# A linear-attention and soft-MoE kernel: combinations four row groups at a time, other PSUM banks in the tail, one DRAM row for k, q, v, and another order

## The chip, the cores and the metric

The kernel runs on one core of a Trainium2 chip. The core has TensorE (PE in the profile, with PEld for its weight loads), VectorE (DVE), ScalarE (ACT), GpSimd (POOL) and SyncE (SP), which here issues every DMA. The metric is the device time of one execution in microseconds (us); lower is better.

## The reference

Two computations follow each other. The first is a gated linear attention over 4 batches, 8 heads, 768 steps and 48 channels; the second is a soft mixture of 8 experts with 4 slots each, over the 3072 rows of 384 channels that the first gives.

```python
B, H, S, D = q.shape                       # 4, 8, 768, 48
f = 1.0 / (1.0 + np.exp(-f_logit))
for t in range(S):
    state = f[:, :, t, :, None] * state + np.einsum('bhd,bhe->bhde', k[:, :, t], v[:, :, t])
    y[:, :, t] = np.einsum('bhd,bhde->bhe', q[:, :, t], state)
x = y.transpose(0, 2, 1, 3).reshape(B * S, H * D)        # 3072 x 384
...
logits = x @ phi                                          # 3072 x 32
d = softmax over rows (columns of slots normalised);  slot_input = d.T @ x
for e in range(E):
    h = np.maximum(slot_input[e] @ w1[e], 0.0)            # 4 x 384 @ 384 x 1024
    slot_out[e] = h @ w2[e]                               # 4 x 1024 @ 1024 x 384
c = softmax of logits over the 32 slots
return c @ slot_out                                       # 3072 x 384
```

Everything is in 32-bit floats.

## The kernel before

**The loop.** The sequence is cut into 24 blocks, `n`, of 128 steps of one batch (6 time blocks times 4 batches, the four batches next to each other). All 8 heads of a block go through together. For each pair of blocks the gates are made: ScalarE exponentiates and takes a logarithm (`exp`, `ln`), VectorE sums logarithms by a scan (`scan`, lines 478 and 479), and ScalarE exponentiates the sum twice (`g` at line 492, `p` at 493). Each block multiplies keys by `g` (`mk`, line 515) and queries by `p` (`mq`, 518). On PE follow: four transposes of the keys (`tk`, 523) with a copy (`pk`, 526), keys by values (`kv`, 544) from which VectorE makes the next state (`sa` 548, `sm` 553), queries by state (`ie`, 563), scores (`sc`, 532), a triangular mask on VectorE (`mask`, 535), masked scores by values (`ia`, 572), a copy of the result (`py`, 575), four transposes (`tx`, 603) and another copy (`px`, 606). After every four blocks a "unit" gathers the logits of 512 rows (line 621), updates a running maximum and the slot sums (lines 625 to 656; the transposes at 642 and their copies at 646 among them).

**After the loop.** The last maxima of four partition groups are joined (724 to 758), the slot inputs are formed (743), and the expert part begins: 12 `up` products of 4 column groups (779), a ReLU (785, 787), 4 groups of four transposes (`tn`, 794) with a copy that masks (800), 12 `down` products in three parts `p` of 128 output channels (`dn`, 813), for each part a scaling (`po`, 821), a sum over head groups (`so`, 825) and a copy (`ps`, 829). Then come the combinations `cb`: for each part, slot outputs by the row softmax for the 3072 rows. A combination of before, `cb{p}{x}`, makes two products, each on 32 rows of the array: partition groups 0 and 32 for even `x`, 64 and 96 for odd `x`. Each result (128 x 768 floats) is copied out (`pf`, 842) and stored (`st`, 845). There are 4 per part, 12 in all. PE also gets idle-time products: `warm` ahead of the loop (417) and `fill` near the end (731).

**Memory.** PSUM is eight banks: three pairs (`pr0` for scores, `pr1` and `pr2` for block results) and two singles (`sg0`, `sg1`) that serve everything of kind "one", the up, turn and down results among it; combinations use the pairs. In SBUF, k, q and v have four buffers each, logits' sums `f` three and decays `c` two groups of two blocks, masked scores two. `w1` is loaded in 12 pieces of 1 MB into `homes` during the loop, paced by the blocks. `w2` has 12 pieces too: three go to homes, seven to the loop's buffers when these come free (`ARENA`), two to homes that the up products have read.

**What sets the order.** A planner (`Plan`, lines 131 to 275) is run while the program is built. Each operation has an estimated time, a priority and, where the table `ENGINE` (line 124) says so, a fixed engine; `LATER` (81) adds to its priority. The planner repeatedly takes the operation that can start first; starts within `WINDOW` of each other count as equal and the priority decides. The program is then written out in that order, and each engine works its list in order. SP too works its DMA list in order: one that waits holds all behind it. Operations with two SBUF operands on VectorE and all on GpSimd are kept from running side by side by explicit waits (lines 937 to 943).

A last operation reads a flag and would run a general, slow path (`general`) if gates were extreme; with these inputs it doesn't run.

Of the kernel before, what the change touches and what calls it, by code (L numbers as in the profile page):

```python
# [16 lines left out]
BT = 128  # L17
# [17 lines left out]
NHOME = 15  # L35
# [37 lines left out]
def t_scan(n):  # L73
# [6 lines left out]
WINDOW = 0.21  # L80
LATER = {
# [5 lines left out]
    "fill": (12.5, 2.9, 4, 21.4, 18.1, 18.3, 19, 14.9), "flag": (0, -14.4, 0.6, -14.5, -18.7, -18.7, -18.7, -18.7),  # L87
# [20 lines left out]
    "scan": (16.7, 12.4, 11.5, 22.8, 22.8, 19.2, 25, 22.8), "sex": (23.7, -22.8, 15.1, 0, 7.3, 7.3, 7.3, 7.3),  # L108
    "si": (-10.5, 0, 0, 0, -23.4, -23.4, -23.4, -23.4), "siv": (13.2, -3.3, 1, 0, -2.2, -2.2, -2.2, -2.2),
    "sm": (-6.5, 16.2, -22.7, 20.8, -10.1, -15.1, 6.1, 2.3), "sml": (-13, 23.5, 8.2, 0, 16.8, 16.8, 16.8, 16.8),  # L110
    "smx": (10, -11.1, -15.3, 0, -10.3, -10.3, -10.3, -10.3),
# [6 lines left out]
    "twb": (-21, 0, 0, 0, -24.1, -24.1, -24.1, -24.1), "twd": (-20.2, 0, 0, 0, -23, -23, -23, -23),  # L118
# [4 lines left out]
}  # L123
# [7 lines left out]
class Plan:  # L131
# [7 lines left out]
    LAT, PE_LAT, SWITCH, DMA_LAT, RATE, DEPTH = 0.13, 0.17, 0.19, 2.0, 375e3, 8  # L139

    INS, PAGE, FETCH = 4, 256, 5.8
# [7 lines left out]
    def add(self, name, eng, fn, r=(), w=(), psum=None, kind=None, prio=0.0, bytes=0, after=(), two=False, form=None, products=0):  # L149

        op = dict(name=name, eng=eng, fn=fn, psum=psum, kind=kind, prio=prio, bytes=bytes, n=len(self.ops), two=two, form=form, products=products)
# [23 lines left out]
    def schedule(self):  # L175
# [24 lines left out]
        while ready:  # L200
            best = None
            for n in ready:
# [8 lines left out]
                for e, us in sorted(op["eng"].items()):  # L211
# [4 lines left out]
                    if e == "SP":  # L216
                        t = max(t, landed[-self.DEPTH])
                    elif e == "POOL" or (op["two"] and e == "DVE"):
                        t = max(t, port if holder == e else port + self.LAT)
                    elif e == "PE" and op["form"] != form:  # L220
                        t = max(t, free.get(e, 0.0) + self.SWITCH)
                    if own is None or t + us < own[1]:
                        own = (t, t + us, op["prio"], n, e)
                if best is None or self.better(own, best):
# [3 lines left out]
            op = ops[n]  # L228
            if e == "PE":
# [10 lines left out]
            if e == "SP":  # L240
                pipe = max(pipe, t + self.DMA_LAT) + op["bytes"] / self.RATE
                end = pipe
                landed.append(end)
# [826 lines left out]
```

## Time and profile before

| | us |
|---|---|
| median of 3 runs | 170.55 |
| lowest and highest run | 169.25 and 171.65 |
| the profiled execution | 169.53 |
| span of its profile | 167.8 |

The profile is of one execution. Its span goes from the first to the last instruction, 1.7 us less than the time of that execution. "Busy" is the time in which an engine had an instruction under way. Matmuls are pipelined, so the mean length of one is longer than the distance to the next; a float product is two passes, and an entry "x4" of PE in the chain counts instructions of that kind. The granted clock is TensorE's, 1.00 for full speed; over this execution it was 0.994 on the mean.

### The profile page before, as it was taken

Reading aid. Unit: us, or ns where it says so; the run is one execution under the profiler, and the core shown is the slowest. Engines: PE = TensorE matmul, PEld = TensorE weight load, DVE = VectorE, ACT = ScalarE, POOL = GpSimd, SP = SyncE. Lnnn points to the kernel's source line nnn. Section 1 sums busy time; section 2 is a strip of 40 time slices with the busy share of each in tenths; the row PEclk is TensorE's granted clock in tenths of the full one; section 3 lists DMA queues with packets and bytes.
Section 4 is the critical chain, followed back from the end, with each engine's and each line's share of the span. In section 5 each row is a group of like instructions: output and inputs, shape, how many; then the busy total and the mean of one; then the engine's idle time right before and its main releaser. Section 6 shows DMA issues by size and latency. Waiting matters only on the chain.

```text
span 167.8 us, 5887 instructions
## 1 busy us (share of the span) xinstructions
PE 153.7 (92%) x2477; PEld 116.3 (69%) x2477; DVE 123.6 (74%) x239; ACT 97.5 (58%) x182; POOL 25.1 (15%) x41
## 2 busy tenths in 40 slices
PE   2998999999999999999999999999989998999940
PEld 2987777688787887788777887787532276857530
DVE  6889979899999999999999999994660162233420
ACT  4998976878689797937985786543302100131300
POOL 3002020230306030321128131500000000000000
PEclk9999999999999999999999999999999999999997
DMA  5999999999999999999999968179999990536680
GB/s 164 349 406 384 407 429 388 355 327 398 395 377 352 355 341 379 364 378 400 401 381 293 357 231 274 68 256 424 422 424 424 410 383 27 191 144 262 241 294 23
DMA packets 17604, 54.02 MB, mean 322 GB/s; under 512 B 1952, under 2 KB 5152, under 8 KB 14496
## 3 DMA queue, kind: packets, MB, share of 16 engines
q1 hardware_dynamic: 17568, 53.55, 84.2%
q8 instruction: 21, 0.34, 0.9%
q14 instruction: 15, 0.12, 0.2%
HBM read 48.82 MB, written 4.72 MB: 319 GB/s over the span
## 4 chain that ended last, share of the span: by engine, by line
PE 63%; DVE 13%; ACT 7%; DMA 7%; issue 3%; SPq 1%; POOL 1%; DVEq 0%; POOLq 0%; ACTq 0%
PE pr L532 11%; PE sg L813 7%; PE sg L779 6%; PE pr L572 6%; PE pr L563 6%; PE sg L603 5%; PE pr L836 5%; DMA ak<-in_k_dram 4%; DVE as L535 4%; PE sg L621 3%; PE sg L523 3%; DMA aq<-in_q_dram 3%; PE sg L650 2%; PE sg L544 2%; ACT ac L493 2%
## 5 line engine op out<-in xcount | busy, mean ns | idle before, releaser
L535 DVE TENSOR_TENSOR as<-pr,tri 128x1024 f32<-128x1024 f32 x24 | 29.2, 1215 | 2.1 <-PE pr L532 1.4
L532 PE MATMUL pr<-aq,ak 48*128 48x128 f32 x384 | 27.9, 285 | 0.4 <-DVE as L535 0.2
L532 PEld LDWEIGHTS pr<-aq,ak 48*128 48x128 f32 x384 | 23.3, 187 | 5.0 <-issue 2.6
L572 PE MATMUL pr<-as,av 128*48 128x128 f32 x384 | 24.1, 274 | 1.1 <-DVE as L535 1.0
L572 PEld LDWEIGHTS pr<-as,av 128*48 128x48 f32 x384 | 20.2, 123 | 2.8 <-DVE as L535 2.0
L603 PE MATMUL sg<-ident,xT 128*128 128x128 f32 x96 | 15.2, 283 | 0.4 <-ACT ag L526 0.2
L518 POOL TENSOR_TENSOR aq<-aq,ac 128x512 f32<-128x512 f32 x9 | 11.4, 1281 | 25.0 <-DMA aq<-in_q_dram 8.7
L575 ACT COPY xT<-pr 128x512 f32<-128x512 f32 x20 | 11.6, 581 | 5.6 <-PE pr L572 5.4
L563 PE MATMUL pr<-aq,st 48*48 48x128 f32 x320 | 13.5, 279 | 0.2 <-DVE aq L518 0.2
L493 ACT ACTIVATE ac<-ac 128x1024 f32<-128x1024 f32 (+1 forms) x13 | 12.9, 993 | 0.5
L515 POOL TENSOR_TENSOR ak<-ak,af 128x512 f32<-128x512 f32 x6 | 7.7, 1281 | 35.4 <-ACT af L492 35.3
L603 PEld LDWEIGHTS sg<-ident,xT 128*128 128x128 f32 x96 | 10.4, 141 | 3.6 <-issue 1.5
L523 PE MATMUL sg<-ident,ak 128*128 128x128 f32 x80 | 11.9, 282 | 0.0
L478 DVE TENSOR_TENSOR_SCAN ac<-chain,af 128x256 f32<-128x256 f32 x16 | 10.9, 682 | 1.0 <-issue 1.0
L526 ACT COPY ag<-sg 128x512 f32<-128x512 f32 x17 | 9.4, 585 | 3.2 <-PE sg L523 3.2
L606 ACT COPY xr<-sg 128x384 f32<-128x384 f32 x17 | 8.1, 480 | 5.3 <-PE sg L603 5.2
L842 DVE COPY hm<-pr 128x768 f32<-128x768 f32 x6 | 5.7, 958 | 7.0 <-PE pr L836 7.0
L563 PEld LDWEIGHTS pr<-aq,st 48*48 48x48 f32 x320 | 8.3, 119 | 3.5 <-issue 2.0
L479 DVE TENSOR_TENSOR_SCAN ac<-chain,af 128x256 f32<-128x256 f32 x16 | 10.7, 667 | 0.0
L779 PE MATMUL sg<-hm,si 128*32 128x512 f32 x96 | 10.5, 593 | 0.1
L544 PEld LDWEIGHTS sg<-av,ag 128*48 128x48 f32 x320 | 8.6, 124 | 2.7 <-issue 1.2
L842 ACT COPY hm<-pr 128x768 f32<-128x768 f32 x6 | 4.8, 799 | 9.8 <-PE pr L836 9.8
(129 smaller groups left out, 254.2 us busy)
## 6 DMA issues: line engine op xcount, KB each, us to landing
hm<-in_w_dram SPq DMA_DIRECT2D x17, 1024.0 KB, 8.1
ak<-in_k_dram SPq DMA_DIRECT2D x24, 256.0 KB, 6.5
aq<-in_q_dram SPq DMA_DIRECT2D x24, 256.0 KB, 6.1
av<-in_v_dram SPq DMA_DIRECT2D x24, 192.0 KB, 5.8
out_dram<-hm SPq DMA_DIRECT2D x12, 384.0 KB, 2.6
af<-in_f_dram SPq DMA_DIRECT2D x7, 512.0 KB, 6.0
ag<-in_f_dram SPq DMA_DIRECT2D x4, 512.0 KB, 6.1
af<-in_w_dram SPq DMA_DIRECT2D x1, 1024.0 KB, 7.0
```

The costliest lines, as they stand in the source:

```text
L493: add(f"p{n}", {"ACT": t_act(w)}, lambda e: nc.scalar.activation(flat(c_), flat(c_), AF.Exp, scale=-1.0), w=cs, prio=T(n, 1.2))
L518: tt(e)(flat(q_), flat(q_), flat(c_), op=ALU.mult)
L523: nc.tensor.transpose(pk[:, a], k_[:, a], ident)
L532: nc.tensor.matmul(ps[:, r, a], k_[rows[r], col(a)], queries(r, a), start=True, stop=True)
L535: tt(e)(sc_.rearrange("p r (m x) t -> p (r m) (x t)", x=2), bank(("sc", n)).rearrange("p r (m t) -> p (r m) t", m=2), tri.rearrange("p x t ...
L544: nc.tensor.matmul(pk[rows[r], col(a)], kp_[:, col(a), rows[r]], v_[:, 2 * a + r], start=True, stop=True)
L563: nc.tensor.matmul(py[at : at + D, r, a // 2], s0[rows[r], col(a)], queries(r, a), start=a < 2, stop=False, skip_group_check=True)
L572: nc.tensor.matmul(py[at : at + D, r, a // 2], v_[:, 2 * a + r], sc_[:, r, a], start=first and a < 2, stop=a >= 2, skip_group_check=True)
L575: copy(e)(xT[:, n % NXT].rearrange("p (r m) t -> p r (m t)", r=2), bank(("y", n))[:, :, : 2 * BT])
L603: nc.tensor.transpose(px[:, i], xT[:, n % NXT, i], ident)
L779: nc.tensor.matmul(ph[32 * qq : 32 * qq + 32], si[:, c], t[:, qq], start=c == 0, stop=c == 2, skip_group_check=True)
L813: nc.tensor.matmul(po[32 * qq : 32 * qq + 32, :w], hT[:, j, 4 * kh + kk, 32 * qq : 32 * qq + 32], t[:, qq, kk], start=(j, kh, kk) == (0, 0 ...
```

## The change

The diff does six things.

1. **Combinations.** A combination now makes four products on all four row groups into one tile of four banks (`halves_`), two of them per part. It has two copies and two stores, as many stores in all as before. All but the last combination use the tile `halves_[1]`; the last uses `halves_[0]`.
2. **Banks in the tail.** PSUM is now two tiles of four banks. The names `pairs` and `ones_` are views of them, in the same sizes as before. The planner gets further pools over the same memory: "late" (the four banks of the second tile) and "spare" (two of the first). Up and turn results may be in "one", "late" or "spare", down results and head sums in "one" or "spare". `fill` is done 4 times in place of 12, from `ident`.
3. **k, q, v.** Host code puts them side by side into one DRAM row of 1408 floats per partition. From block 4 on one DMA loads all three; for blocks 0 to 3 k and q come together and v by itself. There are five buffers for them, four groups of `f`, three of `c` and three of masked scores.
4. **Memory for that.** Two homes fewer (13): one piece of `w2` goes to a home ahead and nine to the loop's buffers. `phi` is loaded over `ones`, once warm-up and `tri` have read it; `wd` and `si` lie over `tri`. The pieces of `w1` and of that first `w2` are loaded in halves, paced over all blocks.
5. **The planner's costs.** Form changes of PE have a price for each form, DMAs a price by row length, some products another length, instruction pages two prices; sums and combinations may be taken 0.3 ahead.
6. **The order.** `WINDOW` is 0, and `LATER` and `ENGINE` are new tables. By `ENGINE` the keys' product `mk` is on GpSimd for all blocks from 4 on (an "A" that an operation can't use leaves the choice to the planner).

```diff
-NHOME = 15
+ROW = 2 * PR * BT + DM
+NHOME = 13
...
-WINDOW = 0.21
+WINDOW = 0
 LATER = {
...
 ENGINE = {
-    "ends": "AA--DDDD", "mk": "--DP-PDA", "mq": "AA--D---", "pc": "PD-PDA--", "pe": "-PA-----", "pf": "AA-AD-P-",
-    "pk": "-AA--P--", "plt": "--D-PPPP", "ps": "D---PPPP", "px": "D-APA-PP", "py": "A-APPPA-", "relu": "AD--PPPP",
-    "sml": "A-------", "ssb": "DPD-DDDD",
+    "ends": "-A--DAAA", "mk": "APADPPPP", "mq": "-PA-PAAP", "pc": "PAPP----", "pe": "ADPPPPPP", "pf": "-P-DAAAP",
+    "pk": "A--AA-AA", "pl": "DP-PDPDD", "plt": "A-AAPAAA", "ps": "AAP-AAAA", "px": "--AP-PDA", "py": "-AP-----",
+    "relu": "-P--AAAA", "sml": "PPP-AAAA", "ssb": "DPP-PPPP",
...
-    LAT, PE_LAT, SWITCH, DMA_LAT, RATE, DEPTH = 0.13, 0.17, 0.19, 2.0, 375e3, 8
+    LAT, PE_LAT, DMA_LAT, DEPTH = 0.13, 0.17, 2.0, 8
+    SWITCH = {"turn": 0.07, "col": 0.1, "row": 0.2, "half": 0.22, "slot": 0.16, "comb": 0.1, "sum": 0.1, None: 0.1}
...
-    pairs = [pp.tile([128, 2, 512], F32, tag=f"pr{i}", name=f"pr{i}") for i in range(3)]
-    ones_ = [pp.tile([128, 512], F32, tag=f"sg{i}", name=f"sg{i}") for i in range(2)]
-    plan = Plan({"sc": [0], "pair": [1, 2], "one": [0, 1]})
+    halves_ = [pp.tile([128, 4, 512], F32, tag=f"pq{i}", name=f"pq{i}") for i in range(2)]
+    pairs = [halves_[0][:, :2], halves_[1][:, :2], halves_[1][:, 2:]]
+    ones_ = [halves_[0][:, 2], halves_[0][:, 3]]
+    plan = Plan({"sc": [0], "pair": [1, 2], "one": [0, 1], "late": [0, 1, 2, 3], "spare": [0, 1], "quad": [1], "last": [0]})
...
-    NF, NK, NQ, NV, NSS, NXT = 3, 4, 4, 4, 5, 6
+    NF, NC, NB_, NSC, NSS, NXT = 4, 3, 5, 3, 5, 6
...
-    phs = part(AV, 1920, 128, a=PR)
+    phs = ones.rearrange("p (a s) -> p a s", a=PR)
...
-        load(kb[n % NK], k[n], f"k{n}", [("k", n % NK)], T(n, -9), 262144)
-        load(qb[n % NQ], q[n], f"q{n}", [("q", n % NQ)], T(n, -8.5), 262144)
-        load(vb[n % NV], v[n], f"v{n}", [("v", n % NV)], T(n, -7), 196608)
+        for name, x in (("kq", slice(0, 1024)), ("v", slice(1024, ROW))) if n < 4 else (("kqv", slice(0, ROW)),):
+            load(bb[n % NB_][:, x], kqv[n, :, x], f"{name}{n}", [("b", n % NB_, c) for c in name], T(n, -7 if name == "v" else -8.5))
...
-        def combine(p, x):
+        def combine(p, h):
             def fn(e):
-                for y in range(2):
-                    gs = slice(64 * (x % 2) + 32 * y, 64 * (x % 2) + 32 * y + 32)
+                for y in range(4):
+                    gs = slice(32 * y, 32 * y + 32)
                     nc.tensor.matmul(
-                        bank(("cb", p, x))[:, y, :384], s4[gs, CUT[p] : CUT[p + 1]], cts[gs, 3 * (x // 2) : 3 * (x // 2) + 3], start=True, stop=True,
+                        bank(("cb", p, h))[:, y, :384], s4[gs, CUT[p] : CUT[p + 1]], cts[gs, 3 * h : 3 * h + 3], start=True, stop=True,
                     )
...
-    add("phs", {"SP": 0.42}, lambda e: nc.sync.dma_start(phs, phi), w=["phs"], prio=T(0, 1), bytes=65536)
+    add("phs", {"SP": 0.42}, lambda e: nc.sync.dma_start(phs, phi), w=["phs", "ones", "warm"], prio=T(0, 1), dma=0.3)
...
-        for x in range(4):
-            h = x // 2
-            add(f"cb{p}{x}", {"PE": 0.4}, combine(p, x), r=[("s4", p), *[("cts", 3 * h + y) for y in range(3)]], psum=("cb", p, x), kind=("pair", "sc"), prio=tp + 2 + 0.1 * x, form="comb", products=2)
...
+        for h in range(2):
+            last = (p, h) == (NPART - 1, 1)
+            add(f"cb{p}{h}", {"PE": 0.65}, combine(p, h), r=[("s4", p), *[("cts", 3 * h + y) for y in range(3)]], psum=("cb", p, h), kind=("last",) if last else ("quad",), prio=tp + 2 + 0.1 * h, form="comb", products=4, ahead=0.3, after=[*ps, *others] if last else ())
+            for x in (2 * h, 2 * h + 1):
+                add(f"pf{p}{x}", {"ACT": t_act(768), "DVE": t_dve(768, True)}, put_f(p, x), psum=("cb", p, h), w=[("st", p, x)], prio=tp + 2.5 + 0.1 * x, after=sdeps[p][x])
```

More of the change, by code (lines that the diff above doesn't have):

```diff
@@ L228, in schedule @@
             op = ops[n]
+            t += op["ahead"]
             if e == "PE":
@@ L278, in gla_soft_moe_kernel @@
 @with_exitstack
-def gla_soft_moe_kernel(ctx: ExitStack, tc: tile.TileContext, q, k, f, v, fd, qd, kd, vd, phi, w1, w2, out):
+def gla_soft_moe_kernel(ctx: ExitStack, tc: tile.TileContext, f, kqv, fd, qd, kd, vd, phi, w1, w2, out):
     nc = tc.nc
@@ L581, in block @@
         if not final:
-            add(f"tk{n}", {"PE": 0.4}, turn_k, r=[K, "ident"], psum=("kt", n), kind=("one",), prio=T(n, 3), form="turn", products=4)
+            add(f"tk{n}", {"PE": 0.48}, turn_k, r=[K, "ident"], psum=("kt", n), kind=("one",), prio=T(n, 3), form="turn", products=2)
             add(f"pk{n}", {"ACT": t_act(512), "DVE": t_dve(512, True)}, put_k, psum=("kt", n), w=[KP], prio=T(n, 3.5))
@@ L672, in unit @@
         for w_ in (1, 0):
-            add(f"te{u}", {"PE": 0.11}, tr(w_), r=[("et", "lt")[w_], "ident"], psum=("el", u, w_), kind=("one",), prio=t0 + 0.6 - 0.1 * w_, form="turn", products=1)
-            add(f"pe{u}", {"ACT": 0.28, "DVE": 0.25}, put_e(w_), psum=("el", u, w_), w=[(("el",), ("ltok", u))[w_]], prio=t0 + 0.8)
-        add(f"pi{u}", {"PE": 0.42}, pins, r=[("el",), *[("x", (n0 + g) % NX) for g in range(UB)]], psum=("pi", u), kind=("one",), prio=t0 + 1, form="slot", products=4)
+            kind = ("e", "l")[w_]
+            add(f"t{kind}{u}", {"PE": 0.2}, tr(w_), r=[("et", "lt")[w_], "ident"], psum=("el", u, w_), kind=("one",), prio=t0 + 0.6 - 0.1 * w_, form="turn", products=0.5)
+            add(f"p{kind}{u}", {"ACT": 0.28, "DVE": 0.25}, put_e(w_), psum=("el", u, w_), w=[(("el",), ("ltok", u))[w_]], prio=t0 + 0.8)
+        add(f"pi{u}", {"PE": 0.62}, pins, r=[("el",), *[("x", (n0 + g) % NX) for g in range(UB)]], psum=("pi", u), kind=("one",), prio=t0 + 1, form="slot", products=4)
         add(f"pp{u}", {"DVE": t_dve(384, True)}, put_p, r=[AL] if u else [], psum=("pi", u), w=["pin"], prio=t0 + 1.2)
@@ L706, in slots @@
         for u in (2 * th, 2 * th + 1):
-            add(f"ct{u}", {"PE": 0.11}, turn(u), r=[L, "ident"], psum=("ct", u), kind=("one",), prio=sp + 0.5, form="turn", products=1)
+            add(f"ct{u}", {"PE": 0.2}, turn(u), r=[L, "ident"], psum=("ct", u), kind=("one",), prio=sp + 0.5, form="turn", products=0.5)
             add(f"pc{u}", {"ACT": 0.28, "DVE": 0.25}, put(u), psum=("ct", u), w=[("cts", u)], prio=sp + 0.6)
@@ L730, in fill @@
         def fill(e):
-            nc.tensor.matmul(bank("fill")[:, 0, :128], ones, ones, start=True, stop=True)
+            nc.tensor.matmul(bank("fill")[:, :128], ident, ident, start=True, stop=True)
         def t_wb(e):
@@ L763, in tail @@
         last = plan.w[("bank", ("lg", L))]
-        for x in range(12):
-            add(f"fill{x}", {"PE": 0.2}, fill, r=["ones"], w=[("bank", "fill")] if x else [], psum="fill", kind=None if x else ("sc",), prio=t0 + 50, form="sum", products=1, after=[last])
+        for x in range(4):
+            add(f"fill{x}", {"PE": 0.2}, fill, r=["ident"], w=[("bank", "fill")] if x else [], psum="fill", kind=None if x else ("spare",), prio=t0 + 50, form="sum", products=1, after=[last])
         add("twb", {"ACT": 0.2}, t_wb, r=["zr1", ("nm", L)], w=["wb"], prio=t0)
-        add("twd", {"DVE": 0.15}, t_wd, r=["wb", "same"], w=["wd"], prio=t0)
+        add("twd", {"DVE": 0.15}, t_wd, r=["wb", "same"], w=["wd", "tri"], prio=t0)
         add("psi", {"PE": 0.21}, psi, r=["wd", "pin"], psum="psi", kind=("one",), prio=t0, form="slot", products=12)
@@ L850, in tail @@
                     x = W1.index((j, hf, c))
-                    add(f"up{j}{hf}{c}", {"PE": 0.86}, up(j, hf, c), r=["si", ("home", x)], w=[("bank", ("up", j, hf))] if c else [], psum=("up", j, hf), kind=None if c else ("one",), prio=t0 + 1 + 0.1 * x, form="slot", products=4)
+                    add(f"up{j}{hf}{c}", {"PE": 0.86}, up(j, hf, c), r=["si", ("home", x)], w=[("bank", ("up", j, hf))] if c else [], psum=("up", j, hf), kind=None if c else ("one", "late", "spare"), prio=t0 + 1 + 0.1 * x, form="slot", products=4)
                 H_ = ("hs", 2 * j + hf)
@@ L917, in gla_soft_moe_kernel @@
         sdeps[p] = [home_deps(x) for x, o in at]
+    ps, others = [], [plan.w["flag"], plan.w["bank", "fill"], *[plan.w["cts", u] for u in range(NU)]]
     for p in range(NPART):
```

138 lines of the change are left out of this document (75 added, 63 removed), and 71 rows, old and new, of the table LATER.

## The prediction

> **What bounds the kernel now.** I read the page first, then the windows by stage, then the chain of waits in order of time, and last the timeline where the chain changes engine.
>
> ```profile
> span 167.8 us, 5887 instructions
> ...
> PE 153.7 (92%) x2477; PEld 116.3 (69%) x2477; DVE 123.6 (74%) x239; ACT 97.5 (58%) x182; POOL 25.1 (15%) x41
> ```
>
> The page says that TensorE (PE) is busy for 92% of the span. That is a mean over unlike stages, so I cut the span where the work changes: until the first scores, until a full flow, the loop, the joint to the expert part, the up products, the turns, the down products, the end, the run-out. Columns: length, then busy us of PE, weight loads, VectorE (DVE), ScalarE (ACT), GpSimd (POOL), then granted clock, DMA share, GB/s.
>
> ```profile
> 0.00:9.60 9.60, 6.50 (x33) 6.38 (x33) 7.03 (x18) 6.90 (x14) 1.67 (x13) 1.00 0.80 279
> 9.60:18.88 9.28, 7.99 (x118) 6.56 (x117) 8.42 (x14) 8.63 (x15) 1.28 (x1) 1.00 1.06 398
> 18.88:112.46 93.58, 92.31 (x1624) 74.17 (x1624) 88.97 (x162) 71.36 (x134) 22.11 (x27) 1.00 0.93 341
> 112.46:123.08 10.62, 9.74 (x139) 6.98 (x135) 6.93 (x25) 3.27 (x10) 0.00 (x0) 1.00 1.01 424
> 123.08:133.51 10.43, 10.43 (x96) 3.01 (x96) 1.98 (x6) 1.40 (x3) 0.00 (x0) 1.00 1.01 420
> 133.51:136.47 2.96, 2.51 (x21) 1.68 (x17) 1.98 (x3) 0.60 (x1) 0.00 (x0) 1.00 1.01 421
> 136.47:154.19 17.72, 17.23 (x420) 13.18 (x419) 5.05 (x9) 3.46 (x5) 0.00 (x0) 1.00 0.45 177
> 154.19:161.15 6.96, 6.96 (x46) 4.33 (x42) 3.22 (x4) 1.86 (x3) 0.00 (x0) 1.00 0.66 254
> 161.15:167.80 6.65, 0.00 (x1) 0.00 (x0) 0.00 (x0) 0.00 (x0) 0.00 (x0) 0.85 0.30 105
> ```
>
> In the loop (93.58 us) PE lacks work for only 93.58 - 92.31 = 1.27 us; DVE is close behind with 88.97. An order can win there only by making the PE work itself shorter, or by 1.27. In the up stage PE is never idle. The rest has slack of another kind: chains of small steps, and combinations.
>
> The chain of waits for the back (start, length, engine and line; L794 turns, L813 down products, L825 head sums, L821 and L829 their copies, L836 combinations; pieces between are left out):
>
> ```profile
> 134.36 0.67 PE sg L794 x4
> 135.87 0.66 PE sg L794 x4
> 136.53 3.69 PE sg L813 x128
> 140.24 0.36 DVE xT L821
> 140.64 0.50 PE sg L825 x2
> 141.17 0.30 DVE xT L829
> 141.51 1.56 PE pr L836 x8
> ...
> 146.70 0.84 PE pr L836 x4
> ...
> 147.97 1.49 PE pr L836 x8
> ...
> 150.47 1.03 PE pr L836 x8
> ...
> 154.26 0.84 PE pr L836 x4
> ...
> 155.97 1.52 PE pr L836 x8
> ```
>
> One old combination is x4 (two products of two passes, two row groups). Its price differs: 0.84 alone, 1.49 to 1.56 for most pairs, but 1.03 for the pair at 150.47.
>
> **Part 1, the combinations, before the last down product.** The old code gives combination x rows 0-63 or 64-127 by x's parity, so a neighbouring pair can occupy all four row groups, which is what one new combination does by design. The pair at 150.47 is therefore the nearest row for it: 1.03. A lower end is 0.84, what two groups cost, if the other two run wholly beside them; an upper end is 1.52, if nothing overlaps. Between 136.47 and 154.19 stand seven old combinations: 1.56 + 0.84 + 1.49 + 1.03 = 4.92 us. There will be four new ones (two each of parts 0 and 1, the seven and the one that now comes at 154.26): at the middle of 0.84 and 1.03, 4 x 0.94 = 3.8. Saved 1.1, between 4.92 - 4 x 0.84 = 1.6 and 4.92 - 4 x 1.52 = -1.2.
>
> The Trainium skill ("TensorE: Matmul & The Clock Gate", Part 3) gives two figures: a span of one matmul plus 4 ns for each further tile, and a measured 3.07 times for four row tiles. By the first a new combination would cost 0.84 and part 1 save 1.6; by the second four products take 1.3 times one (0.65 by 1.49 - 0.84, so 0.85, and the same 0.2 of switching ahead: 1.04) and it saves 0.8. The pair at 150.47 speaks for the second.
>
> From 140.24 to 141.51 lie 0.36 + 0.30 us of DVE copies and about 0.1 at each handover, with only two small transposes of PE work beside them. With down products of part 1 there instead (their weights: part 3 below), about 0.8 is hidden; one or two more returns to the down form cost 0.2. Term A: 1.1 + 0.8 - 0.2 = 1.7; bounds -1.2 and 2.4.
>
> **Part 2, after the last down product.** Here the stores answer, not the combinations.
>
> ```profile
> out_dram<-hm SPq DMA_DIRECT2D x12, 384.0 KB, 2.6
> 159.00:160.00 1.00, 1.00 (x8) 0.46 (x6) 0.33 (x1) 0.80 (x1) 0.00 (x0) 1.00 1.01 396
> 159.67 0.96 DVE L842 COPY hm<-pr 128x768 f32<-128x768 f32 x1 [1.18 <-PE pr L836]
> L842 ACT COPY hm<-pr 128x768 f32<-128x768 f32 x6 | 4.8, 799 | 9.8 <-PE pr L836 9.8
> ```
>
> Before: last down product ends at 154.26, last copy at 159.67 + 0.96 = 160.63, its store lands 2.6 later, at 163.2, or 9.0 after the down product. The remaining 4.6 us to 167.80 hold no engine work and stay. After: copy 0.36, sum 0.50, copy 0.30, handovers 0.3: the first new combination starts 1.5 later and ends at 2.4, ScalarE copies 0.8, to 3.3. From then four stores of 393 KB follow each other, at the 396 GB/s that a full DMA second shows 0.99 us each: 3.3 + 2.6 + 3 x 0.99 = 8.9. By the engines alone it would be 2.4 + 0.94 + 0.96 + 2.6 = 6.9. Term: 0.1, bounds -0.5 and 2.1.
>
> **Part 3, from the up products to the down products.** The up products end at 133.5, the down products start at 136.47. Of the 2.96 us between, four groups of turns take 2.51 busy; they run there because the up results held the two single banks. With six more banks for up and turn results, three groups of turns can go between up products and three of part 0's four down products before the last turn. The turns remain PE work, now with a form change more each way. I take 0.7 saved; bounds 0 and 1.6 (0.45 idle, and the 1.1 that overlapping turns with each other showed as 0.67 each).
>
> The weights of the down products must keep up:
>
> ```profile
> 100.72 0.33 SPq L440 DMA_DIRECT2D af<-in_w_dram  x1
> ...
> 125.92 2.04 SPq L440 DMA_DIRECT2D hm<-in_w_dram  x2
> ```
>
> Two homes less means one piece of w2 loaded early instead of three, but before, too, the first piece of w2 went out at 100.72 and the last two at 125.92, and the DMA ran at 420 GB/s to 136.47. The same 12 MB follow the loop, spots in the same number; the last two are used near 151. Cost 0; should they come 10 us later, the PE would wait for what exceeds 15.
>
> **Part 4, the joint (10.62 us, PE idle 0.88).** One wait there is the order's:
>
> ```profile
> 119.95 0.14 PEld L642 LDWEIGHTS sg<-ident,av 128*128 128x128 f32 x1 [0.26 <-DVE zr L727]
> ```
>
> The transpose that feeds the slot sums waits for the bank of another small product, though its exponentials are done. A new order may shed that: 0.4, bounds -0.5 and 0.9. Twelve filling products become four; they fill waits, cost 0, and if their cover goes, each costs under 0.2.
>
> **Part 5, the loop.** Arithmetic, shapes and counts are unchanged. What an order changes are PE's form changes:
>
> ```profile
> 48.75 0.59 PE sg L523 x4
> 49.33 0.44 PE sg L603 x4
> ```
>
> Four transposes take 0.59 behind another form and 0.44 behind transposes: 0.15 a merge. There are 44 such groups (20 of keys, 24 of outputs), so 22 merges, some of them there already, are at most 3.3 us; the score and state products can hardly pair up, with one bank pair for scores. Adding the 1.27 idle, the upper bound is 4.5; the lower is -1.5, an order that merges less. A third copy of scores and of decays and a fifth of k, q, v give freedom, as does DVE, which sheds work:
>
> ```profile
> L515 POOL TENSOR_TENSOR ak<-ak,af 128x512 f32<-128x512 f32 x6 | 7.7, 1281 | 35.4 <-ACT af L492 35.3
> L515 DVE TENSOR_TENSOR ak<-ak,af 128x512 f32<-128x512 f32 x10 | 6.8, 683 | 0.6 <-DMA ak<-in_k_dram 0.6
> L515 DVE TENSOR_TENSOR ak<-ak,ag 128x512 f32<-128x512 f32 x6 | 4.1, 687 | 0.1
> 16.93 1.29 DVE L518 TENSOR_TENSOR aq<-aq,ac 128x512 f32<-128x512 f32 x2 [0.21 <-POOL ak L515]
> ```
>
> The new table pins the key product of every block from 4 on to POOL. Of the 16 on DVE, three belong to blocks 0, 1 and 3; the other 13 leave, 13 x 0.685 = 8.9 us, and DVE's loop falls from 88.97 to 80. So DVE stops being the second bound, unless it waits for POOL (rival C). I take a third of the 4.5: 1.5 saved; bounds -1.5 and 4.5.
>
> **Part 6, the start.** The first scores begin at 9.60, and up to 18.88 PE idles 1.29.
>
> ```profile
> 3.10 6.56 PE L417 MATMUL sg<-ones 128*128 128x128 f32 x32 [3.10 <-DVE ones L375]
> 9.31 0.33 SPq L861 DMA_DIRECT2D av<-in_phi_dram  x1
> ```
>
> The warm-up ends at 9.66 and is kept, so the first scores keep their place. Keys, queries and values as one row make fewer, longer lines (5.6 KB for 2 and 1.5), while the page of before shows the DMA at 398 GB/s here already: it may save the 1.29. Against it stands a new wait. The phi load now overwrites the warm-up's operand, so it waits on SP's queue until 9.66, where the plan books that warm-up at 8 x 0.3 = 2.4 us against 6.56. Everything behind it on SP waits too: the rows of blocks 3 and later. In 9.66 us at 279 GB/s 2.7 MB land, about what is issued ahead of it (f and k, q, v of blocks 0 to 2); a gap of the length of one landing, some 2 us, can follow. Term 0; bounds -2 and 1.3.
>
> **Sum.** 1.7 + 0.1 + 0.7 + 0.4 + 1.5 + 0 = 4.4. The profiled execution took 169.53 (1.7 outside its span of 167.8): 165.1. It lies 1.0 below the median of the runs, 170.55, and inside their 169.25 to 171.65; I keep **165.0**.
>
> **Rivals.**
>
> A, **the loop gives what it can**: 4.0 of part 5's 4.5 and the start's 1.3 come in: 165.0 - 2.5 - 1.3 = 161.2. For it: DVE's relief and the deeper buffers, at a stage where PE is idle for 1.4% only because its work is long. Against it: DVE at 95% had hardly delayed PE at all.
>
> B, **the back doesn't shorten**: there is one four-bank tile for all new combinations but the last, and it is free only after both copies. The second combination of a part then waits 0.96 + 0.2; if no down product lies between, for parts 0 and 1 that is 2 x 1.2 = 2.4, and the loop's 1.5 are lost as well with an order built for other costs: 165.0 + 2.4 = 167.4, or 168.9 with both. For it: PE works its list in order. Against it: twelve groups of down products, 0.92 each by 3.69 / 4, lie around. The Trainium skill ("TensorEngine Tiling (Array Packing)", PSUM Bottleneck) warns of this: once tiles run side by side, copying out of PSUM may become the limit. In the trace before, the copies left both engines mostly idle there (DVE 5.05 and ACT 3.46 of 17.72).
>
> C, **POOL makes the loop wait, and it ends slower.** At least 30 loop products run on POOL (20 of keys, 10 of queries pinned) instead of 17, each 1.281 against 0.685. A DVE operation with two SBUF operands may not run beside one, and the mask, the state and the copies queue behind it on DVE; PE waits for the mask. DVE has 93.6 - 80 = 13.6 us to spare: it decides from 13.6 / 30 = 0.45 us of waiting per POOL product. Half a product, 0.64, makes 19.2, so 5.6 over; without the loop's 1.5 that is 165.0 + 7.1 = 172.1. Two thirds, 0.85, make 25.5 and 178.4; I price it between, at 175. For it: POOL's product is nearly twice as long. Against it: the waits shown are 0.21 and shorter, and the scores have a third buffer.
>
> **Chances.** Forecast 0.50 (its own range 162.5 to 167.4), A 0.22, B 0.18, C 0.10. About 2% is what a measurement of this kernel tells from no change: faster means below 167.1, slower above 174.0. Forecast and A lie below, but for 0.04 of the forecast at its upper end: faster 0.68. B and that are the same: 0.22, and with the low end of C that stays under 174, 0.25. Slower: the rest of C, 0.07. The range for 8 in 10 runs from 160.8, just under A, to 169.2, just over B with both its losses; C and the outermost sums are left out.
>
> **What would show it.** Part 1: the group of combinations x16, near 0.94 per four products, and the stage of down products at 15.9 instead of 17.7. Part 2: four stores back to back after the last copies, about 9 us from the last down product to the last landing. Part 3: turns between up products. Part 5: PE's loop shorter by 1 to 2 us with more groups of transposes x8, POOL over 38 us, DVE near 80. Part 6: the phi issue at 9.7 and whether DMA pauses behind it. I am wrong if combinations show 1.5 each, if the loop is longer, or if DVE's wait for POOL passes 0.45 a product.

## The result, and the profile after

The changed kernel takes **272.57 us** (271.81 to 274.39), the kernel before 169.94 beside it: a ratio of 1.603, interval 1.588 to 1.618. The forecast was 165.0 with a range from 160.8 to 169.2. It was wrong by 107.6 us, and on the wrong side. The profiled execution took 274.39, its span is 272.6. Where some executions of one program lie more than 1.5% above its fastest, at a lower granted clock, the times and differences below are those of the others, and a range of times in brackets is that of all.

The head of the page of the changed kernel:

```profile
span 272.6 us, 5764 instructions
...
PE 192.1 (70%) x2461; PEld 141.0 (52%) x2461; DVE 113.8 (42%) x215; ACT 99.1 (36%) x183; POOL 51.5 (19%) x64
...
PE   5756785777876868677767775967766569888740
...
PEclk9998599568598597956559555689989959999995
```

PE has 16 instructions fewer than before and is busy 38 us longer; the rest, 66 us, is PE idle. Hardly a slice reaches 9 tenths (the mean of before was 92%), and the granted clock goes up and down between 0.5 and 0.9.

The windows of the changed kernel, cut at the same events as in the prediction (start, until the third scores, loop to the last scores, joint, up products, turns, down products, last combinations, run-out; same columns):

```profile
0.00:9.32 9.32, 6.41 (x36) 6.24 (x36) 6.49 (x17) 6.61 (x13) 1.65 (x13) 1.00 0.76 252
9.32:24.01 14.69, 8.48 (x145) 6.89 (x144) 9.66 (x16) 10.26 (x17) 3.77 (x3) 1.00 1.03 411
24.01:202.04 178.03, 129.93 (x1578) 100.55 (x1578) 83.52 (x151) 68.04 (x126) 44.81 (x46) 0.73 0.53 192
202.04:223.69 21.65, 14.57 (x151) 9.43 (x151) 5.44 (x17) 4.31 (x13) 0.61 (x1) 0.82 0.29 108
223.69:236.27 12.58, 11.85 (x97) 3.01 (x98) 0.65 (x3) 2.04 (x4) 0.61 (x1) 0.91 0.77 301
236.27:240.11 3.84, 2.40 (x17) 1.73 (x18) 2.13 (x4) 0.86 (x2) 0.00 (x0) 1.00 0.28 115
240.11:257.82 17.71, 15.29 (x414) 11.94 (x414) 3.50 (x7) 3.19 (x6) 0.00 (x0) 1.00 0.24 92
257.82:262.27 4.45, 3.17 (x30) 1.24 (x26) 1.46 (x3) 2.26 (x3) 0.00 (x0) 1.00 0.64 251
262.27:272.60 10.33, 0.00 (x0) 0.00 (x0) 0.96 (x1) 1.54 (x3) 0.00 (x0) 0.73 0.54 204
```

The loop went from 93.58 to 178.03. Of these 84.5 us, 37.6 are PE busy longer (129.93 against 92.31, at a clock of 0.73) and 46.8 are PE idle (48.1 against 1.3). The joint lost another 11.0, the start 5.1, the run-out 3.7, the up products 2.2, the turns 0.9. Only the stretch with the new combinations got shorter: 240.11 to 262.27 is 22.2, and was 24.7.

What PE and the engines that read its results wait for. The view of waits (engine, line, "<-" releaser: us in all, times, longest), and seven us of the loop in the timeline (start, length, engine, line; in brackets the idle time before and what ended it):

```profile
ACT ag L544 <- PE pq L550: 15.7, 4, 8.1
...
PEld pq L621 <- DVE as L553: 9.4, 5, 2.7
DVE hm L862 <- ACT hm L862: 9.1, 4, 3.8
DVE ab L553 <- PE pq L621: 9.0, 3, 5.8
```

```profile
53.02 2.08 PE L550 MATMUL pq<-ab 48*128 48x128 f32 x16 [0.57 <-DVE ltok L664]
55.14 0.56 DVE L674 COPY pin<-pq 128x384 f32<-128x384 f32 x1 [2.27 <-PE pq L550]
...
55.75 1.97 PE L541 MATMUL pq<-ident,ab 128*128 128x128 f32 x8 [0.65 <-DVE pin L674]
56.21 0.67 DVE L497 TENSOR_TENSOR_SCAN ac<-chain,af 128x256 f32<-128x256 f32 x1
...
57.75 1.22 DVE L553 TENSOR_TENSOR as<-pq,tri 128x1024 f32<-128x1024 f32 x1 [0.88 <-PE pq L541]
...
59.01 1.07 ACT L544 COPY ag<-pq 128x512 f32<-128x512 f32 x2 [7.78 <-DVE as L553]
...
60.14 0.56 PE L562 MATMUL pq<-ab,ag 128*48 128x48 f32 x16 [0.88 <-ACT ag L544]
```

The pairs of the first view have no data in common, and the timeline has three more such waits. (The wait of L562 for L544 is for data, and that of L541 for L674 can be for a bank that is used again.) The copy of slot sums (L674) reads its own bank, and waits for scores (L550) that go to two others. The scores end at 55.10; when VectorE has done two scans, at 56.88, their mask (L553) could start, but it waits another 0.88, until the key transposes (L541), in yet other banks, end at 57.72. ScalarE's copy of those transposes (L544) then waits for the mask to end at 58.97, although both only read PSUM. All of them go to one tile, `pq0`: the scores' pair and the two singles are views of it now. In these rows an access of one engine is held behind earlier accesses of the others to other banks of the tile, so the engines take turns where they had worked side by side.

At the end, where a combination's two copies read different pairs of one tile, the same shows with nothing else around it:

```profile
248.85 0.80 ACT L862 COPY hm<-pq 128x768 f32<-128x768 f32 x1 [1.05 <-PE pq L855]
```

```profile
249.69 0.96 DVE L862 COPY hm<-pq 128x768 f32<-128x768 f32 x1 [1.49 <-ACT hm L862]
```

VectorE starts 0.04 us after ScalarE has ended (248.85 + 0.80).

The Trainium skill ("PSUM — Partial Sum Buffer", "PSUM bank collisions raise a hardware error") says that no two engines may access one bank and quadrant at the same time, not even two readers, and asks to guard PSUM by bank and quadrant. A guard, that is waits that keep such accesses apart, orders two readers too if it follows that rule. No run here shows a collision; the waits above show a guard as wide as the tile, four banks. The experiments below ask whether that is the cause of the lost time.

### The profile page after: what moved, and what is told of

It reads as the page before. It is cut to its first block, busy times and chain, and to the rows that moved or that the text cites. A ratio compares the mean times of both kernels' runs of the same rounds, so it can differ in the third digit from the quotient of the medians.

```text
span 272.6 us, 5764 instructions
## 1 busy us (share of the span) xinstructions
PE 192.1 (70%) x2461; PEld 141.0 (52%) x2461; DVE 113.8 (42%) x215; ACT 99.1 (36%) x183; POOL 51.5 (19%) x64
## 4 chain that ended last, share of the span: by engine, by line
PE 56%; DVE 20%; ACT 10%; issue 5%; DMA 3%; POOL 1%; SPq 1%; DVEq 0%; ACTq 0%; POOLq 0%
PE pq L550 12%; PE pq L590 9%; DVE as L553 6%; PE pq L541 6%; PE pq L621 6%; PE pq L798 4%; PE pq L832 3%; DVE ab L553 3%; PE pq L639 3%; DMA af<-in_f_dram 3%; PE pq L668 3%; PE pq L581 2%; PE pq L562 2%; ACT ag L544 2%; DVE st L571 2%
## 5 line engine op out<-in xcount | busy, mean ns | idle before, releaser
L550 PE MATMUL pq<-ab 48*128 48x128 f32 x384 | 37.6, 351 | 6.4 <-DVE xr L624 2.0
L550 PEld LDWEIGHTS pq<-ab 48*128 48x128 f32 x384 | 32.1, 248 | 12.7 <-issue 5.6
L553 DVE TENSOR_TENSOR as<-pq,tri 128x1024 f32<-128x1024 f32 x16 | 19.5, 1222 | 23.8 <-PE pq L639 6.9
L621 PE MATMUL pq<-ident,xT 128*128 128x128 f32 x96 | 18.0, 321 | 15.3 <-DVE as L553 7.1
L541 PE MATMUL pq<-ident,ab 128*128 128x128 f32 x80 | 18.3, 384 | 14.7 <-DVE as L553 4.9
L544 ACT COPY ag<-pq 128x512 f32<-128x512 f32 x20 | 11.1, 586 | 40.8 <-PE pq L550 15.7
L590 PE MATMUL pq<-as,ab 128*48 128x128 f32 x256 | 23.8, 349 | 1.3 <-DVE as L553 1.3
L533 POOL TENSOR_TENSOR ab<-ab,af 128x512 f32<-128x512 f32 x10 | 12.7, 1271 | 63.0 <-ACT af L510 37.5
L541 PEld LDWEIGHTS pq<-ident,ab 128*128 128x128 f32 x80 | 13.2, 196 | 18.7 <-DVE as L553 6.2
L590 PEld LDWEIGHTS pq<-as,ab 128*48 128x48 f32 x256 | 18.7, 159 | 5.1 <-issue 3.2
L581 PE MATMUL pq<-ab,st 48*48 48x128 f32 x320 | 15.7, 323 | 1.7 <-issue 1.1
L562 PE MATMUL pq<-ab,ag 128*48 128x48 f32 x320 | 12.7, 244 | 4.8 <-ACT ag L544 2.8
L562 PEld LDWEIGHTS pq<-ab,ag 128*48 128x48 f32 x320 | 11.8, 158 | 7.3 <-ACT ag L544 3.9
L553 DVE TENSOR_TENSOR ab<-pq,tri 128x1024 f32<-128x1024 f32 x8 | 9.8, 1221 | 10.5 <-PE pq L621 9.0
```

The costliest lines, as they stand in the source:

```text
L533: tt(e)(flat(k_), flat(k_), flat(g_), op=ALU.mult)
L541: nc.tensor.transpose(pk[:, a], k_[:, a], ident)
L544: copy(e)(flat(kp_), bank(("kt", n)))
L550: nc.tensor.matmul(ps[:, r, a], k_[rows[r], col(a)], queries(r, a), start=True, stop=True)
L553: tt(e)(sc_.rearrange("p r (m x) t -> p (r m) (x t)", x=2), bank(("sc", n)).rearrange("p r (m t) -> p (r m) t", m=2), tri.rearrange("p x t ...
L562: nc.tensor.matmul(pk[rows[r], col(a)], kp_[:, col(a), rows[r]], v_[:, 2 * a + r], start=True, stop=True)
```

## The experiments

**One tile or several (a_split).** The changed kernel with its order, rows and engines, and the same eight banks as five tiles:

```diff
-    halves_ = [pp.tile([128, 4, 512], F32, tag=f"pq{i}", name=f"pq{i}") for i in range(2)]
-    pairs = [halves_[0][:, :2], halves_[1][:, :2], halves_[1][:, 2:]]
-    ones_ = [halves_[0][:, 2], halves_[0][:, 3]]
+    pairs = [pp.tile([128, 2, 512], F32, tag="pr0", name="pr0")]
+    ones_ = [pp.tile([128, 512], F32, tag=f"sg{i}", name=f"sg{i}") for i in range(2)]
+    pairs += [pp.tile([128, 2, 512], F32, tag=f"pr{i}", name=f"pr{i}") for i in (1, 2)]
```

A combination writes into pairs 1 and 2; the last one into pair 0 and the singles, so that its second copy becomes two of 384.

> The changed kernel with every use of PSUM in a tile of its own again (one pair for scores, two pairs for block results, two singles); a four-row-group combination writes into two pairs, the last one into a pair and the two singles (its second copy becomes two). Order, tables, k/q/v row, SBUF and DMAs as in the changed kernel. Theory 1 (operations on different banks of one shared PSUM tile are made to wait for each other, PE loses work and then its clock): 160 to 168 us, PE idle in the loop below 4 us, granted clock above 0.98. Theory 2 (the key products on GpSimd hold up DVE, rival C of the prediction): no change, 260 to 275. Theory 3 (the new order, or k, q, v, a mask result in one SBUF tile): no change, 260 to 275.

Measured: 172.6 (172.43 to 177.21), beside 169.33 for the kernel before. 100 of the 103 us are gone, as the first theory said; its figure, 160 to 168, was missed by 4.6, and what is left is taken up below. The windows of its profile (span 171.1, execution 172.81), at the same events, the last two lines being what follows the last down product:

```profile
0.00:9.67 9.67, 7.01 (x36) 6.84 (x36) 6.37 (x17) 6.69 (x13) 2.32 (x14) 1.00 0.81 291
9.67:21.44 11.77, 8.63 (x146) 6.96 (x145) 9.71 (x16) 9.97 (x16) 3.11 (x3) 1.00 1.03 409
21.44:116.81 95.37, 92.44 (x1578) 74.36 (x1578) 81.79 (x151) 66.79 (x126) 45.26 (x46) 0.98 0.95 355
116.81:128.44 11.63, 10.86 (x156) 8.04 (x152) 5.62 (x18) 4.50 (x13) 0.61 (x1) 1.00 0.79 295
128.44:138.94 10.50, 10.50 (x97) 3.08 (x98) 0.64 (x3) 1.96 (x4) 0.61 (x1) 1.00 0.81 313
138.94:141.54 2.60, 2.23 (x18) 1.76 (x18) 1.34 (x3) 0.86 (x2) 0.00 (x0) 1.00 0.85 353
141.54:158.00 16.46, 15.17 (x416) 11.96 (x416) 4.95 (x8) 3.10 (x6) 0.00 (x0) 1.00 0.23 88
158.00:161.50 3.50, 3.12 (x30) 1.34 (x26) 1.31 (x5) 2.20 (x3) 0.00 (x0) 1.00 0.96 372
161.50:171.10 9.60, 0.06 (x4) 0.00 (x0) 0.42 (x1) 1.59 (x3) 0.00 (x0) 0.71 0.59 223
```

The same 1578 PE instructions of the loop take 95.37 us, at a clock of 0.98; VectorE and ScalarE do the same work in both (83.52 and 81.79, 68.04 and 66.79). The key, query and value buffers are one SBUF tile here as well, so that sharing cost nothing of this size. And the two copies of a combination, which took turns above, now run side by side:

```profile
150.20 0.80 ACT L871 COPY hm<-pr 128x768 f32<-128x768 f32 x1 [1.01 <-PE pr L859]
```

```profile
150.26 0.96 DVE L871 COPY hm<-pr 128x768 f32<-128x768 f32 x1 [0.87 <-PE pr L859]
```

**The other way round (b_merge).** The kernel before, with nothing changed but its five tiles made views of two, by the three lines marked "-" above.

> The kernel before with one edit: its five PSUM tiles become views of two tiles of four banks, as in the changed kernel; nothing else. Theory 1: 240 to 290 us, granted clock near 0.8. Theories 2 and 3: 168 to 172, as before.

Measured: 287.15 (two executions, 285.49 and 288.81), ratio 1.691 (1.675 to 1.707).

```profile
span 287.1 us, 5886 instructions
...
PE 202.5 (71%) x2477; PEld 147.6 (51%) x2477; DVE 126.7 (44%) x239; ACT 98.4 (34%) x182; POOL 24.9 (9%) x41
```

Three lines, with the old combinations, rows, order and engines, cost 118 us. The shared tile alone is enough. GpSimd (POOL) is at its old load, so its products are not needed for it.

**Which of the two tiles (a_split0, a_split1).** Only the first taken apart (scores and singles), and only the second (the pairs of block results).

> As a_split, but only the first shared tile is taken apart (scores and the two singles); block results and four-bank combinations still share the second tile. Theory 1: most of the loss comes back, since scores, transposes, key-value products and all their copies lived in the first tile: 165 to 200 us. Theories 2 and 3: 260 to 275.

> As a_split, but only the second shared tile is taken apart (the two pairs of block results); scores and the two singles still share the first. Theory 1: little comes back, 235 to 268 us. Theories 2 and 3: 260 to 275.

Measured, one execution each: 178.6 and 264.04. The first tile carries nearly all of it. With the second alone shared, 178.6 stands against 172.6 for a_split, whose executions go up to 177.21, so one execution does not settle what the second costs. The first holds the scores, which are read by a 1.22 us mask, and everything that passes through the singles.

**The combinations alone (c1_comb).** The kernel before, with six combinations of four products into its pairs 1 and 2:

```diff
-                for y in range(2):
-                    gs = slice(64 * (x % 2) + 32 * y, 64 * (x % 2) + 32 * y + 32)
+                for y in range(4):
+                    gs = slice(32 * y, 32 * y + 32)
```

> The kernel before with one part of the change: six combinations of four products on four row groups, written into the two pairs of block results (separate tiles), old tables, old costs. If four row groups run side by side (0.93 us for four products, as in a_split), the stretch from the first down product to the last combination falls from 23.2 us to about 20 and the stores at the end give back 1 to 1.5: 167 to 168.5 us. If the copies out of the one set of banks pace it instead, 169 to 171.

Measured: 168.22 (167.88 to 168.99), ratio 0.9926 (0.9894 to 0.9959), a gain whose interval leaves out 1, though it is under the 2% that the prediction took to tell a change from none. Two stretches of its profile (the down products; what follows the last of them) and the last combinations:

```profile
136.57:152.06 15.49, 15.00 (x419) 12.02 (x418) 3.13 (x7) 4.07 (x6) 0.00 (x0) 1.00 0.41 158
152.06:166.70 14.64, 5.43 (x49) 3.49 (x46) 3.22 (x4) 2.57 (x4) 0.00 (x0) 0.81 0.58 219
```

```profile
154.17 0.93 PE L842 MATMUL pr<-ltok,xT 32*128 32x384 f32 x8
156.57 0.93 PE L842 MATMUL pr<-ltok,xT 32*128 32x384 f32 x8
```

A combination of four products lasts 0.93, and the stretch of down products 15.49 instead of 17.72. What comes behind is 14.64 instead of 13.6: the last combination stands 2.40 behind the one before it, whose two copies must empty the same banks. So of 2.2 won, 1.2 stays.

**With more banks for up, turn and down results (c3_comb_banks).** c1_comb with "late" and "spare" as in the change, over separate tiles.

> c1_comb, and up, turn and down results and head sums may use the six further banks. If turns between up products save what the prediction took (0.7 us, bounds 0 and 1.6): 0 to 1.5 us below c1_comb, about 167 us. If the transposes' extra form changes cost as much: equal to c1_comb.

Measured: 170.78 (170.70 to 172.20), ratio 1.011 (1.005 to 1.017). That is 2.6 above c1_comb; neither expectation had it.

```profile
122.97:139.71 16.74, 14.83 (x125) 5.90 (x125) 5.04 (x11) 2.15 (x5) 0.00 (x0) 1.00 0.91 369
139.71:154.79 15.08, 14.60 (x413) 11.71 (x412) 2.24 (x5) 3.80 (x5) 0.00 (x0) 1.00 0.33 127
```

With banks to spare, the planner put turns between the up products, and PE waited there for their ReLUs: from the first up product to the first down product it took 16.74, before 13.39. PE's idle time there is 1.91, and was 0.45; the rest is more PE work in this stretch, 14.83 for 12.94, filling products among it. In the order of the change (a_split) the same way takes 13.10, but there no turn stands between the up products: they run 10.50 without a gap, as before.

**The last combination in other banks (c4_last).** c1_comb with the change's other bank rule: the last combination uses the scores' pair and the two singles.

> This is c1_comb (the kernel before with six combinations of four products) with one thing more of the change: the last combination takes the scores' pair and the two single banks, so that it does not wait for the copies of the one before it. In c1_comb the last combination starts at 156.57, 2.40 behind the one before it (154.17), because it waits for two copies (0.96 and 0.80) of the same banks. Theory (the wait for banks is what the tail lost): it starts about 0.9 behind the other, near 155.1, and the copies end 1 us or more earlier; the stores, 0.99 each, then bind, so the time is 0.3 to 1.2 lower than c1_comb: 167.0 to 167.9, ratio 0.985 to 0.991. Rival (the stores bind already): unchanged, 168.2, ratio 0.992 to 0.994.

Measured: **167.41** (166.96 to 169.91, ten executions), ratio **0.9888** (0.9842 to 0.9933). This is below both kernels; against the one before it is 1.1%, with an interval that leaves out 1, and still under the 2%. The last two combinations of its profile, the first of them now the one in the other banks:

```profile
153.73 0.59 PE L844 MATMUL pr<-ltok,xT 32*128 32x384 f32 x2
...
154.48 0.82 PE L844 MATMUL pr<-ltok,xT 32*128 32x384 f32 x8
```

They end at 155.30 instead of 157.50, and the span is 165.7 instead of 166.7. Not all of this is the banks' doing: the down products, ahead of which nothing was changed, start 0.45 earlier in this execution (136.12 and 136.57). Counted from there, the combinations end 1.75 earlier and the program 0.55, so about a third arrived.

**What a_split still lacks.** 171.1 of span against 167.8 is 3.3, by the windows: start +2.6 (third scores at 21.44 and 18.88), loop +1.8, joint +1.0, up and turns -0.3, down products -1.3, the end -0.5. Three runs are about the first two.

d_phi: a_split, with the warm-up multiplying `ident` so that the phi load needn't wait for it.

> a_split, but the warm-up multiplies another operand, so that the phi load no longer waits for it on SP's queue (9.38 us in a_split); nothing else. Theory 1 (that wait, and the loads of gates and rows queued behind it, make the start of a_split late: third scores at 21.4 us against 18.9 before): third scores near 19, 2 to 3 us saved, 169 to 171.5. Theory 2 (the start is late by the planned order of ScalarE's work, not by loads): third scores stay above 20.5, 172 to 175.

Measured: 173.4 (173.24 to 178.20; the profiled execution took 178.20), ratio 1.025 (1.020 to 1.031). The phi load moved from 9.38 to 5.88, and the time is not below a_split's 172.6; the third scores start at 21.82 in the profile, no earlier than in a_split. The wait is there and is not what costs, as the second theory said; that ScalarE's order is what costs, its other half, is not shown.

e_start: d_phi, with five operations moved in the written order.

```diff
+    for name, place, after in (("exp4", "g2", 0), ("p2", "g2", 1), ("mq2", "mk3", 1), ("mq3", "mq2", 1), ("sc2", "kv2", 0)):
+        plan.order.remove(at[name])
+        plan.order.insert(plan.order.index(at[place]) + after, at[name])
```

> This is d_phi (the changed kernel with its PSUM in separate tiles, the phi load free of the warm-up) with five operations moved in the written order at the start: the third pair's exponentials (exp4) ahead of g2, p2 right behind g2, the query products mq2 and mq3 behind mk3, and the third scores ahead of the key-value products kv2. In a_split the third scores start at 21.44, against 18.88 in the kernel before, after a wait of 1.12 for the query product on DVE, which waits for p2 on ACT at 19.58 (15.56 in the kernel before). Theory (2 to 2.6 of what a_split lacks is this order at the start): the third scores start at 20.0 or earlier and the time is 1.3 to 2.5 lower than d_phi's 173.4: 170.9 to 172.1. Rival (the loop is bound by a later engine, so an earlier third block only waits later): the third scores are earlier, but the time stays at 172.8 to 174.5.

Measured: 173.86 (173.86 to 178.92, four executions, of which the profiled one took 177.21). No gain on d_phi's 173.4: the theory missed, and the rival's 172.8 to 174.5 holds the fastest execution alone. In the profile the third scores are earlier, the fourth are not (24.65 in a_split):

```profile
19.36 1.38 PE L545 MATMUL sg<-ident,ab 128*128 128x128 f32 x8 [1.40 <-POOL ab L537]
20.68 1.16 PE L554 MATMUL pr<-ab 48*128 48x128 f32 x16
...
26.13 1.12 PE L545 MATMUL sg<-ident,ab 128*128 128x128 f32 x4 [1.59 <-POOL ab L537]
27.18 2.08 PE L554 MATMUL pr<-ab 48*128 48x128 f32 x16
```

Moving exp4 ahead of g2 made g2 later (it starts at 16.92, in a_split at 15.07), and with it POOL's key products, on which PE now waits. A move by hand pays one wait with another there; it does not show where a_split's 2.6 us come from.

b_port: the kernel before, with the new entries for the key and query products in `ENGINE` alone.

```diff
-    "ends": "AA--DDDD", "mk": "--DP-PDA", "mq": "AA--D---",
+    "ends": "AA--DDDD", "mk": "APADPPPP", "mq": "-PA-PAAP",
```

> The kernel before with the new fixed engines for the key and query products alone (the key product of every block from 4 on on POOL, and three of four query products free or on POOL as in the new table); PSUM, combinations, rows and all priorities as before. Theory of the prediction's part 5 (relief of DVE lets the loop run closer to PE): POOL over 38 us busy, DVE under 115, the loop 0 to 1.5 shorter, 168 to 169.5. Rival C of the prediction (POOL's products, 1.28 each, make the loop wait): PE idles more in the loop, 172 to 178. Third possibility (priorities that were searched for other engines): 170 to 173 with the idle time of PE spread over many releasers and not on POOL.

Measured: 189.29 in the fastest of four executions (189.29 to 203.92), 19.6 above the kernel before. The profiled execution took 197.06; from it a line of the page, one stretch and one wait:

```profile
PE 166.5 (85%) x2477; PEld 123.2 (63%) x2477; DVE 116.0 (59%) x224; ACT 97.6 (50%) x176; POOL 50.2 (26%) x62
```

```profile
100.00:120.00 20.00, 17.07 (x177) 12.87 (x177) 11.18 (x20) 6.62 (x12) 3.77 (x3) 0.66 0.42 136
```

```profile
PE sg L523 <- POOL ak L515: 0.9, 1, 0.9
```

All three expectations are far below even the fastest. In the profile PE is idle 28.8 us (195.3 less 166.5), 14.7 more than before, and busy 12.8 longer, with the clock at 0.66 in the stretch shown. The waits of PE that POOL itself ends are small: the one above and one of 0.7. PE's waits are spread over many lines, as the third possibility said, but at several times its price. That priorities searched for one division of work do not fit another would explain it, and is not shown by itself. In a_split POOL is as busy (51.9), and this loss is not there.

## Why the prediction was wrong, and where it was right

**The step that failed is one that has no term in the sum: the banks.** The prediction read the change to PSUM only as a gain of places ("with six more banks for up and turn results", Part 3) and as a limit on combinations (rival B). That `pairs` and `ones_` became views of two tiles was taken to be a change of names, at nothing, and without the sentence that an edit at nothing needs: what covers it, and what it costs if the cover is gone. b_merge prices it at 118 us in the old kernel, a_split at 100 in the new one. No trace of before could show the wait, since there every bank group is a tile of its own; so it had to be bounded. The rows of before allow it, those of the mask and of the copy of key transposes:

```profile
L535 DVE TENSOR_TENSOR as<-pr,tri 128x1024 f32<-128x1024 f32 x24 | 29.2, 1215 | 2.1 <-PE pr L532 1.4
...
L526 ACT COPY ag<-sg 128x512 f32<-128x512 f32 x17 | 9.4, 585 | 3.2 <-PE sg L523 3.2
```

If PE has to stop in each of 24 blocks for one of each, that is 24 x (1.215 + 0.585) = 43 us (an estimate from these two rows), where the loop's idle time grew by 46.8. A rival with that price would have been on the right side.

The other 37.6 us of the loop were in no part of the prediction either: PE at a mean clock of 0.73, which came with the idle time and is gone with it in a_split (0.98).

The steps that were priced can be read in a_split and c1_comb, where the shared tiles are gone:

- **Part 1** has its price right: a new combination was to take 0.94, and takes 0.93. The stretch of down products was to take 15.9 (16.0 by the part's own sum), and takes 15.49 in c1_comb, 16.46 in the order of the change. That this is near is partly luck. Three new combinations stand in it, not four: the fourth starts as the last down product ends. And the 0.8 of handovers to be hidden are not hidden: PE idles 0.49 in the stretch before and in c1_comb, and 1.29 in a_split. The two estimates worked out there from figures of the Trainium skill ("TensorE: Matmul & The Clock Gate", Part 3) bracket it: 0.84 by the one, 1.04 by the other.
- **Part 2** held. From the last down product to the end, 8.9 + 4.6 = 13.5 was said; a_split shows 171.1 - 158.0 = 13.1. With the combinations of c1_comb, which all share one set of banks, it is 14.6.
- **Part 3** was to give 0.7, and gave 0.3. Its picture, turns between up products, is not in the new order; where the planner did it (c3_comb_banks) that stretch was 3.35 longer.
- **Part 4** was to give 0.4, and cost 1.0, outside its lower bound of -0.5.
- **Part 5** has its loads right: DVE 81.79 in the loop where 80 was said, POOL 51.9 where over 38 was. Its gain is wrong: the loop is 1.8 longer, not 1.5 shorter, outside its lower bound of -1.5. PE's work did not get shorter by merged form changes (92.44 busy, 92.31 before), its idle time grew from 1.27 to 2.93, and no gain from DVE's relief is to be seen.
- **Part 6** was put at 0 within -2 and 1.3; it cost 2.6. The wait of the phi load came as described (issued at 9.38) and no pause of the DMA with it (share 1.03 until 21.44), and d_phi shows that it is not the cost. The lower bound is passed all the same.

Added up, the parts give a_split a span 3.3 longer than before, where 4.4 less was forecast: even without the shared tiles the time, 172.6, would have been above the range of the forecast, by the loop and the start. Why the new order is slower there stays open; the two moves that were tried did not settle it.

**Rival A** is refuted by that loop. **Rival B** has one half there once, at the last combination of c1_comb (2.40; freed of it in c4_last, the program gained about 0.55), and not at the others, which down products cover as its counterargument said; its other half, the loop's gain lost with an order built for other costs, is what a_split's loop looks like. **Rival C** named the right side with the wrong mechanism: in a_split VectorE's query products wait 1.9 us for POOL in three waits, far from 13.6. b_port shows that the same division of work can cost 20 us in an order that was made for another.

## What to carry to other kernels

When a diff turns separate on-chip tiles into views of one, ask how wide the guard of that memory is, and price it as if every reader and writer of the tile took turns; here that was 100 to 118 us on 170. (A shared SBUF tile showed nothing of this size.) Look for waits between operations that share no data but a tile's name: they are the signature. And don't judge a table of engines and priorities that was searched as a whole by some of its entries in another: b_port lost 20 us by two.

## What the runs showed of the hardware

The granted clock fell although no wait was long. In the loop of the changed kernel PE is busy for 73% of the time, and its longest wait is this one:

```profile
151.49 1.97 PE L541 MATMUL pq<-ident,ab 128*128 128x128 f32 x8 [1.76 <-ACT xr L624]
```

Yet the clock is 0.73 over the loop, and 0.59 in these seven us, in which PE is idle for 1.41 in all:

```profile
53.00:60.00 7.00, 5.59 (x40) 4.71 (x40) 3.98 (x6) 0.99 (x3) 0.00 (x0) 0.59 0.00 1
```

One group of scores takes 1.16 at full clock and 2.08 there. In a_split's loop, with PE busy for 97% of it, the clock is 0.98. So idle time in pieces came with nearly as much again in slower work: 37.6 us of busy time beside 46.8 of idle time. The Trainium skill ("TensorE: Matmul & The Clock Gate", Part 1) says that the clock is halved after an idle window of about 3.4 us; its section "A second HAM failure mode: psum-queue depth-cycling" adds that frequent short idle times between groups do it too. This case agrees with the second: 1.76 is the longest wait of PE in that loop, and the clock fell. How much idle time is too much, no run here shows.
